# A Fourier mixing layer with a feed-forward block: the first unit's transform by direct tables, and folds at other steps

## The chip, the cores and the metric

The kernel runs on one core of a Trainium2 chip. The metric is the device time of one execution in microseconds (us). In the text, TensorE is the matrix engine (PE in the profile, PEld its weight loads), DVE the vector engine, ACT the scalar engine, GpSimd is POOL, and SyncE (SP) issues the transfers.

## The reference

The input `x` has 8 samples of 3008 rows and 256 columns. A two-dimensional Fourier transform is taken per sample, its real part goes through two matrix products with a leaky ReLU between them.

```python
X = np.fft.fft(x, axis=1)              # x: (8, 3008, 256)
X = np.fft.fft(X, axis=2)
x = X.real.astype(np.float32).reshape(24064, 256)
h = x @ w_in                           # w_in: (256, 2048)
g = np.maximum(0.01 * h, h)
out = (g @ w_out).astype(np.float32)   # w_out: (2048, 256)
```

The kernel gets the weights as 64-bit floats and converts them itself (`begin`, `mantissa`, `end`: bit operations on DVE and ACT).

## The kernel before

The transform along the 3008 rows uses symmetries. Rows are laid out in 8 chunks of up to 95 rows (`ROWS`), each beside its mirror image, in two halves `h`. The *folds* add and subtract mirrored rows and columns, so that a small matrix of cosines or sines remains. A *unit* is one sample `b` and one parity `c` of the output frequencies; there are 16 units, the first is `(0, 1)`. Each unit has two parts: cosines (part 0) and sines (part 1). The column in the middle of the features (the Nyquist column) is treated apart, for all 8 samples at once.

```python
def add_mirrors(t, h, rows):
    a, z = t[:, h, 0, rows], t[:, h, 1, rows]
    nc.vector.tensor_tensor(a, a, z, op=ALU.add)

def fold_columns(t, h, part, rows, v=nc.vector):
    a, z = t[:, h, 0, rows], t[:, h, 1, rows]
    if part == 0:
        nc.vector.tensor_tensor(z[:, :, 0:P], a[:, :, 0:P], a[:, :, P:D], op=ALU.add)
    else:
        v.tensor_tensor(z[:, :, P + 1 : D], a[:, :, 1:P], a[:, :, P + 1 : D], op=ALU.subtract)
        nc.gpsimd.memset(z[:, :, P : P + 1], 0.0)

def fold_halves(t, part, c, rows, to=None, v=nc.vector):     # one halving
    ...
    v.tensor_tensor(to, z[:, 0], z[:, 1], op=(ALU.add, ALU.subtract)[i])

def fold_x(b, h):                       # a later sample, one half of it
    add_mirrors(t, h, rows)
    for part in range(2):
        fold_columns(t, h, part, rows)
    if h == 1:
        for part in range(2):
            for c in PARITIES:
                fold_halves(t, part, c, rows)
```

For parity 1 a further fold needs *turns*: pairs of chunks are turned by an angle, which is two or four scalings on ACT and two sums on DVE or GpSimd.

```python
def turn(x, y, a, part, tmp, to, v):
    nc.scalar.activation(tmp[0], y, ACT.Copy, scale=sin)
    nc.scalar.activation(tmp[1], y, ACT.Copy, scale=cos)
    if v is nc.vector:
        v.scalar_tensor_tensor(to[0], in0=x, scalar=cos, in1=tmp[0], op0=ALU.mult, op1=op[part])
        v.scalar_tensor_tensor(to[1], in0=x, scalar=sin, in1=tmp[1], op0=ALU.mult, op1=op[1 - part])
        return
    nc.scalar.activation(to[0], x, ACT.Copy, scale=cos)
    nc.scalar.activation(to[1], x, ACT.Copy, scale=sin)
    v.tensor_tensor(to[0], to[0], tmp[0], op=op[part])
    v.tensor_tensor(to[1], to[1], tmp[1], op=op[1 - part])
```

After the folds, `even_rows` and `odd_rows` multiply four chunks each with a table of 95 columns per chunk into a bank of the sum memory (PSUM), and `butterfly` on DVE puts the banks together into `mix`, the transformed block of 752 columns that the first matrix product reads.

The opening, for the first unit (cut):

```python
w = load_w_in(0, half)
nc.sync.dma_start(nyx, x_nyq)
nc.sync.dma_start(angle, angle_tab)
load_rows(0, evens)                    # a quarter of the sample, 1 MB
for n in range(2):
    load_tab(n, 1)
load_rows(1, evens)
for h in range(2):
    load_rows(h, odds)
nc.sync.dma_start(feat_sb, ...)
for n in range(2, 4):
    load_tab(n, 1)
o = load_w_out(0)
convert(w)
fold_nyquist()
nyq = nyquist_rows(1)
...
add_mirrors(t, 0, evens)
fold_columns(t, 0, 0, evens)
fold_columns(t, 0, 1, evens, nc.gpsimd)
keep_warm(17)                          # matmuls on zeroes
nyq = mix_nyquist(nyq, nc.gpsimd)
... # the other folds, turns and products, on DVE, GpSimd and ACT
fold_halves(t, 1, 1, odds, v=nc.gpsimd)
sine.fold_odd(nc.gpsimd)
...
even, odd = mix(units[0], 1)
even(even_sines)
odd(odd_rows(sine, P))
o.begin()
o.mantissa()
```

After the opening come steps. A step `(j, f)` takes a chunk of 251 columns of `mix` through two blocks of hidden columns: `up` (four matmuls, then DVE and ACT make `g`), and three steps later `down` (seven matmuls with sums made by GpSimd; at the chunk's last `f`, seven adds on DVE that empty the four sum banks). Between them the folds and transforms of the unit to come are put in:

```python
if 0 < n < len(units) - 1:
    ...
    if part == 0 and n % 2 == 1 and f in (2, 5):
        fold_x(b + 1, f // 5)
    if part > 0 and f == 1:
        fold_rows(units[n + 1], part - 1)
    if part > 0 and f == 4:
        dft(units[n + 1], part - 1)
...
if at - lag >= done:
    down(*steps[at - lag])             # lag = 3
```

Of the kernel before, what the change touches and what calls it, by code (L numbers as in the profile page):

```python
# [53 lines left out]
F32 = mybir.dt.float32  # L56
# [6 lines left out]
P = 128  # L63
# [11 lines left out]
KB = [47, 94]  # L75

PARITIES = (1, 0)

# [51 lines left out]
def seq_tables():  # L130

    out = np.zeros((4, 2, P, TW[0][1]), np.float32)
    rows = row_order()

# [18 lines left out]
    for part in range(2):  # L153
# [19 lines left out]
        out[2 * part + 1, 0, :, : TW[0][1]] = np.concatenate([values(4, fours)[part], values(4, eights)[part], p, q], axis=1)  # L173
    return out

# [51 lines left out]
def tile_fnet_leaky_relu(  # L227
# [5 lines left out]
    w_out: bass.AP,  # L233
    seq_tab: bass.AP,
    angle_tab: bass.AP,
    feat_tab: bass.AP,
# [13 lines left out]
    def dft_ps():  # L250
        return up_ps("dft_ps")
# [13 lines left out]

    def fold_columns(t, h, part, rows, v=nc.vector):

        a, z = t[:, h, 0, rows], t[:, h, 1, rows]
        if part == 0:
            nc.vector.tensor_tensor(z[:, :, 0:P], a[:, :, 0:P], a[:, :, P:D], op=ALU.add)  # L270
        else:
            v.tensor_tensor(z[:, :, P + 1 : D], a[:, :, 1:P], a[:, :, P + 1 : D], op=ALU.subtract)  # L272
            nc.gpsimd.memset(z[:, :, P : P + 1], 0.0)

    def fold_halves(t, part, c, rows, to=None, v=nc.vector):

        i, cols = (c + part) % 2, slice(part * P, (part + 1) * P)
        z = t[:, :, 1, rows, cols]
        to = t[:, i, 0, rows, cols] if to is None else to[:, rows]
        v.tensor_tensor(to, z[:, 0], z[:, 1], op=(ALU.add, ALU.subtract)[i])  # L280

    def fold_x(b, h):

        t, rows = xs[b], slice(0, NT)
        add_mirrors(t, h, rows)
        for part in range(2):
            fold_columns(t, h, part, rows)
        if h == 1:
            for part in range(2):
                for c in PARITIES:  # L290
                    fold_halves(t, part, c, rows)
            zs[b] = xs.pop(b)
# [56 lines left out]
    def rows_of_x(b, part, c):  # L349

        t = zs[b]
        src = t[:, (c + part) % 2, 0, :, part * P : (part + 1) * P]
        return Rows(src, [t[:, part, 1].rearrange("p c (i d) -> p (c i) d", i=2)], part, c)


# [171 lines left out]

    def butterfly(to, m, part, c, v=nc.vector):

# [15 lines left out]

        banks = []

        def copied(bank, at, w):

            banks.append(bank)  # L550
            a = work.tile([P, 384], F32, tag="e0", bufs=2, name="e0")
            if v is nc.vector:
                nc.scalar.copy(a[0:m, 0:w], bank[0:m, at : at + w])
                return a, bank
            used = 4 * ROWS if bank is banks[0] else 4 * n + 2
            nc.scalar.copy(a[0:m, 0:used], bank[0:m, 0:used])
            return a[:, at:], a

        def even(pe):
            if c == 1:  # L560
                e0, pe = copied(pe, 0, 2 * ROWS)
                x, y = two(e0, 0, ROWS, ROWS), two(pe, 2 * ROWS, ROWS, ROWS)
                v.tensor_tensor(four(ab)[:, 0::2], x[:, :, 1:], y[:, :, 1:], op=ALU.add)
                either(four(ab)[:, 1], x[:, 0, 1:], y[:, 0, 1:])
                v.tensor_tensor(four(ab)[:, 3], x[:, 1, 0:n][:, ::-1], y[:, 1, 0:n][:, ::-1], op=ALU.subtract)
                v.tensor_tensor(ev[0:m, 0 : 2 * n], ab[0:m, 0 : 2 * n], ab[0:m, 2 * n : 4 * n], op=ALU.add)
                either(ev[0:m, 2 * n : 4 * n], ab[0:m, 0 : 2 * n], ab[0:m, 2 * n : 4 * n])
                return
# [6 lines left out]

        def odd(po):
            if c == 1:
                q = 2 * n + 1
# [5 lines left out]
                return  # L584
            direct = od[0:m, n : n + 378].rearrange("p (a n) -> p a n", a=2)[:, :, 0:188]
            nc.scalar.copy(direct.rearrange("p a (b n) -> p b a n", b=2)[:, :, :, 0:48],
                           po[0:m, 0:192].rearrange("p (b a n) -> p b a n", b=2, a=2))
# [11 lines left out]

    def mix(u, blk):  # L600

        t = work.tile([P, UW[0]], F32, tag=f"mix{blk}", bufs=2, name=f"mix{blk}")
        mixed.setdefault(u, {})[blk] = t
        return butterfly(t, P, blk, u[1])

# [14 lines left out]

    def nyquist_rows(c):
        rows = Rows(nya[:, c], [nyz], 0, c)
        rows.fold_even(nc.gpsimd)
        rows.fold_odd(nc.gpsimd)
        return rows

    def mix_nyquist(rows, v):
        c = rows.c
        banks = even_rows(rows, B), odd_rows(rows, B)
        t = work.tile([P, UW[0]], F32, tag="mix0", bufs=2, name="nyq")  # L630
        for made, bank in zip(butterfly(t, B, 0, c, v), banks):
            made(bank)
        nc.sync.dma_start(nyq_dram[:, c, 0 : UW[c]], t[0:B, 0 : UW[c]])
        return t
# [116 lines left out]
    def step(at):  # L751
        if at < len(steps):
# [6 lines left out]
            if 0 < n < len(units) - 1:  # L759
                if part == 0 and f == 4:  # L760
                    spread(units[n + 1])
                if part == 0 and n % 2 == 1 and f in (2, 5):
                    fold_x(b + 1, f // 5)
                if part > 0 and f == 1:
                    fold_rows(units[n + 1], part - 1)
                if part > 0 and f == 4:
                    dft(units[n + 1], part - 1)
# [14 lines left out]
    with tc.manual_schedule(engines={mybir.EngineType.DVE, mybir.EngineType.PE, mybir.EngineType.SP}):  # L782
        with tc.manual_schedule(engines={mybir.EngineType.Pool, mybir.EngineType.Activation}):
# [16 lines left out]
            w = load_w_in(0, half)  # L800
            nc.sync.dma_start(nyx, x_nyq)
            nc.sync.dma_start(angle, angle_tab)
            load_rows(0, evens)
            for n in range(2):
                load_tab(n, 1)
            load_rows(1, evens)
            for h in range(2):
                load_rows(h, odds)
            nc.sync.dma_start(feat_sb, feat_tab.rearrange("(a p) n -> p a n", p=P))
            for n in range(2, 4):  # L810
                load_tab(n, 1)
            o = load_w_out(0)
            convert(w)
            fold_nyquist()
            nyq = nyquist_rows(1)

            def blocks_of(tag, name):
                return work.tile([P, 2 * WN], F32, tag=tag, bufs=dict(s=4, g=5)[tag], name=name).rearrange("p (c d) -> p c d", d=P)

            differences = blocks_of("s", "differences")  # L820
            cosine, sine = (Rows(src, [blocks_of("g", "folded") for _ in range(2)], part, 1)
                            for part, src in enumerate((differences, t[:, 0, 0, :, P:D])))
            add_mirrors(t, 0, evens)
            fold_columns(t, 0, 0, evens)
            fold_columns(t, 0, 1, evens, nc.gpsimd)
            keep_warm(17)
            nyq = mix_nyquist(nyq, nc.gpsimd)
            add_mirrors(t, 1, evens)
            fold_columns(t, 1, 0, evens)
            fold_columns(t, 1, 1, evens)  # L830
            fold_halves(t, 0, 1, evens, differences)
            cosine.fold_even()
            fold_halves(t, 1, 1, evens)
            keep_warm(8)
            even_cosines = even_rows(cosine, P)
            sine.fold_even(nc.gpsimd)
            for h in range(2):
                add_mirrors(t, h, odds)
                fold_columns(t, h, 0, odds)
                fold_columns(t, h, 1, odds, (nc.vector, nc.gpsimd)[h])  # L840
            fold_halves(t, 0, 1, odds, differences)
            cosine.fold_odd()
            fold_w_in(0, half, w, "sum")
            w, w1 = load_w_in(half, half), load_w_in(WN, WN)
            even_sines = even_rows(sine, P)
            even, odd = mix(units[0], 0)
            even(even_cosines)
            fold_halves(t, 1, 1, odds, v=nc.gpsimd)
            sine.fold_odd(nc.gpsimd)
            zs[0] = t  # L850
            odd_cosines = odd_rows(cosine, P)
            odd(odd_cosines)
            spread_first(nyq)
            even, odd = mix(units[0], 1)
            even(even_sines)
            odd(odd_rows(sine, P))
            o.begin()
            o.mantissa()
            nyq = nyquist_rows(0)
        with tc.manual_schedule(engines={mybir.EngineType.Activation}):  # L860

# [3 lines left out]
            o1 = load_w_out(1)  # L865
            for n in range(4):
                load_tab(n, 0)
            up(*steps[1])
# [50 lines left out]
        for part in range(2):  # L919
            fold_rows(units[1], part)  # L920
    mix_nyquist(nyq, nc.vector)
    spread(units[1])
# [35 lines left out]
```

## Time and profile before

| | |
|---|---|
| time, median of 3 | 1918.74 us (1918.53 to 1919.8) |
| profiled span | 1917.6 us |
| busy TensorE, DVE, GpSimd, ACT | 1898.6, 1293.5, 1136.7, 514.1 us |
| mean granted TensorE clock | 0.994 |
| moved by transfers | 76.01 MB, mean 40 GB/s |

Lines of the profile name the line of the kernel (L672), the engine, the operation, what is written and read (out<-in), and a count (x4). A note in brackets tells the idle time before the instruction and what ended it. In a timeline the first two numbers are start and duration in us. In a list of waits they are the total, the number of times and the longest wait. In the kernel before, L264 is `add_mirrors`, L270 and L272 `fold_columns`, L280 `fold_halves`, L298 to L307 the turns, L524 the products of the transform, L582 and L583 the two last instructions of `mix` for the first unit, L672 the matmuls of `up`, L735 those of `down`, L746 the seven adds and L780 the matmuls on zeroes. A matmul on 32-bit floats has two records.

### The profile page before, as it was taken

The page shows a single profiled execution, that of the slowest core. Times are in us where ns is not written, and L with a number is a line of the kernel's source. Part 1 is how long each engine was busy: PE and PEld are TensorE (multiplying, and loading weights), DVE is VectorE, ACT ScalarE, POOL GpSimd, SP SyncE. Part 2 cuts the span into 40 slices and gives each one's busy share as a digit, 9 for nine tenths or more (in the row PEclk, how much of TensorE's full clock was granted, in tenths as well). Part 3 has the DMA queues.
Part 4 walks back from the last instruction along what each step waited for, and adds up shares of the span by engine and source line. Part 5 has one row for each costly group of instructions (what it writes and reads, how often), then busy time and mean ns, then how long its engine had stood idle before and what let it go on. Part 6 is the DMA issues. An engine that isn't in the chain of part 4 may idle for free.

```text
span 1917.6 us, 25461 instructions
## 1 busy us (share of the span) xinstructions
PE 1898.6 (99%) x9132; PEld 1689.9 (88%) x9132; DVE 1293.5 (67%) x2580; ACT 514.1 (27%) x721; POOL 1136.7 (59%) x1551
## 2 busy tenths in 40 slices
PE   8999999999999999999999999999999999999999
PEld 6789888888889888888888988889888888888988
DVE  7878855697556966569655796558864587556554
ACT  4532322222222322223222232222322222222221
POOL 5117655576555865558655675557655576555554
PEclk7999999999999999999999999999999999999999
DMA  5313000020001100020000200002000030000000
GB/s 190 104 31 118 12 20 12 22 107 12 20 22 59 60 12 31 12 99 20 18 25 12 107 12 23 19 12 107 22 12 20 11 118 12 20 12 22 11 11 22
DMA packets 26876, 76.01 MB, mean 40 GB/s; under 512 B 4976, under 2 KB 18672, under 8 KB 24960
## 3 DMA queue, kind: packets, MB, share of 16 engines
q1 hardware_dynamic: 25600, 74.40, 10.4%
q8 instruction: 73, 1.20, 0.3%
q14 instruction: 51, 0.42, 0.1%
q10 hardware_dynamic: 1152, 0.00, 0.0%
HBM read 49.68 MB, written 24.71 MB: 39 GB/s over the span
## 4 chain that ended last, share of the span: by engine, by line
PE 92%; DVE 4%; issue 1%; DMA 0%; ACTq 0%; ACT 0%; DVEq 0%; SPq 0%
PE sum_ps L735 54%; PE cos_ps L672 16%; PE sin_ps L672 16%; PE dft_ps L524 3%; PE sum_ps L715 2%; DVE g L681 1%; DVE cos L677 1%; DVE g L682 1%; DVE xt L280 1%; DVE xt L272 0%; DMA xt<-in_x_dram 0%; PE wf_ps L468 0%; DVE xt L264 0%; DVE e L746 0%; ACTq L477 0%
## 5 line engine op out<-in xcount | busy, mean ns | idle before, releaser
L683 ACT ACTIVATE g<-g 128x1004 f32<-128x1004 f32 (+1 forms) x384 | 399.3, 1040 | 1096.1 <-DVE g L682 1022.6
L677 DVE SCALAR_TENSOR_TENSOR cos<-nb,wn,cos_ps 128x251 f32<-128x251 f32 (+1 forms) x768 | 329.6, 470 | 522.4 <-PE cos_ps L672 521.8
L690 POOL TENSOR_TENSOR s<-g 128x251 f32<-128x251 f32 (+1 forms) x368 | 283.5, 770 | 659.5 <-ACT g L683 659.5
L735 PE MATMUL sum_ps<-s,wt 128*128 128x251 f32 (+1 forms) x2208 | 529.0, 374 | 3.3 <-DVE e L746 3.3
L735 PEld LDWEIGHTS sum_ps<-s,wt 128*128 128x128 f32 x2208 | 415.4, 188 | 57.5 <-issue 5.3
L672 PE MATMUL cos_ps<-mix,wf 128*128 128x251 f32 (+1 forms) x1536 | 391.0, 376 | 1.8 <-ACT wf L470 1.8
L672 PE MATMUL sin_ps<-mix,wf 128*128 128x251 f32 (+1 forms) x1536 | 388.8, 375 | 0.2 <-DVE mix L582 0.2
L735 PE MATMUL sum_ps<-g,wo 128*128 128x251 f32 (+1 forms) x1472 | 373.1, 375 | 0.5 <-DVE o L746 0.5
L672 PEld LDWEIGHTS cos_ps<-mix,wf 128*128 128x128 f32 x1536 | 292.0, 190 | 36.9 <-ACT wf L470 2.8
L672 PEld LDWEIGHTS sin_ps<-mix,wf 128*128 128x128 f32 x1536 | 291.1, 190 | 35.9 <-PE cos_ps L672 0.8
L691 POOL TENSOR_TENSOR s<-s,g 128x251 f32<-128x251 f32 (+1 forms) x368 | 318.6, 866 | 0.0
L735 PEld LDWEIGHTS sum_ps<-g,wo 128*128 128x128 f32 x1472 | 276.9, 190 | 32.7 <-DVE o L746 1.3
L693 POOL TENSOR_TENSOR s<-g,s 128x251 f32<-128x251 f32 (+1 forms) x368 | 279.7, 760 | 28.9
L681 DVE TENSOR_TENSOR g<-cos,sin_ps 128x502 f32<-128x502 f32 (+1 forms) x384 | 259.4, 675 | 44.5 <-DVE cos L677 8.0
L682 DVE TENSOR_TENSOR g<-cos,sin_ps 128x502 f32<-128x502 f32 (+1 forms) x384 | 257.0, 669 | 0.0
L692 POOL TENSOR_TENSOR s<-g 128x251 f32<-128x251 f32 (+1 forms) x368 | 251.0, 682 | 0.0
L735 PE MATMUL sum_ps<-g,wt 128*128 128x251 f32 (+1 forms) x736 | 215.8, 375 | 0.0
L735 PE MATMUL sum_ps<-s,wo 128*128 128x251 f32 (+1 forms) x736 | 215.8, 375 | 0.0
L735 PEld LDWEIGHTS sum_ps<-s,wo 128*128 128x128 f32 x736 | 139.4, 189 | 16.4
L735 PEld LDWEIGHTS sum_ps<-g,wt 128*128 128x128 f32 x736 | 139.8, 190 | 15.8
L746 DVE TENSOR_TENSOR o<-e,sum_ps 128x251 f32<-128x251 f32 (+1 forms) x184 | 67.4, 408 | 8.7 <-ACT e L744 8.7
L524 PEld LDWEIGHTS dft_ps<-tab,xt 95*128 95x128 f32 x484 | 59.2, 192 | 1.6
(133 smaller groups left out, 892.3 us busy)
## 6 DMA issues: line engine op xcount, KB each, us to landing
xt<-in_x_dram SPq DMA_DIRECT2D x14, 2048.0 KB, 9.8
out_dram<-o SPq DMA_DIRECT2D x80, 251.0 KB, 2.3
xt<-in_x_dram SPq DMA_DIRECT2D x4, 1024.0 KB, 9.5
raw<-in_w_out_dram SPq DMA_DIRECT2D x8, 512.0 KB, 4.4
out_dram<-o SPq DMA_DIRECT2D x16, 250.0 KB, 2.2
raw<-in_w_in_dram SPq DMA_DIRECT2D x6, 512.0 KB, 5.0
nb<-nyq_dram SPq DMA_DIRECT2D x8, 376.5 KB, 3.4
nb<-nyq_dram SPq DMA_DIRECT2D x7, 376.0 KB
```

Source lines behind the costliest of these rows:

```text
L524: nc.tensor.matmul(o, lhsT=still, rhs=moving, start=(i == 0), stop=(i == 3), skip_group_check=True)
L672: nc.tensor.matmul(pt[blk][:, h * n : (h + 1) * n], lhsT=wf[:, blk, fs[h] * P : (fs[h] + 1) * P], rhs=mixed[b, c][blk][:, at : at + n], st ...
L677: nc.vector.scalar_tensor_tensor(cos[:, hs], in0=spreads[b, c][:, at : at + n], scalar=wn[:, fs[h] : fs[h] + 1], in1=pt[0][:, hs], op0=ALU ...
L681: nc.vector.tensor_tensor(g[:, 0], cos[:, 0 : 2 * n], pt[1][:, 0 : 2 * n], op=ALU.add)
L682: nc.vector.tensor_tensor(g[:, 1], cos[:, 0 : 2 * n], pt[1][:, 0 : 2 * n], op=ALU.subtract)
L683: nc.scalar.activation(g, g, ACT.Lrelu)
L690: nc.gpsimd.tensor_tensor(s1, a[1][0], a[1][1], op=ALU.add)
L691: nc.gpsimd.tensor_tensor(s2, s1, a[0][0], op=ALU.subtract)
L692: nc.gpsimd.tensor_tensor(s3, a[0][0], a[1][0], op=ALU.subtract)
L693: nc.gpsimd.tensor_tensor(s4, a[0][1], s2, op=ALU.subtract)
L735: nc.tensor.matmul(sums[j][p], lhsT=still[p], rhs=moving[p], start=(f == 0 and i % 2 == 0), stop=(f == NH - 1), skip_group_check=True)
L746: nc.vector.tensor_tensor(to, x, y, op=ALU.add)
```

## The change

The first unit and its part of the Nyquist column are transformed without turns: new tables (`direct_tab`, 1.06 MB for each part) hold full cosines and sines for each chunk, so the folded chunks go straight to TensorE. All folds of `x` run on DVE; the zeroing of a column that is zero already goes. The loads are reordered: the tables come in three pieces between the quarters of `x`, the old tables of parity 1 are loaded later. More matmuls on zeroes keep TensorE running. For later samples the folds are put at other steps, away from the step in which a chunk ends. The aim is a shorter opening with TensorE at full clock, and no waits for the seven adds.

```diff
+    class Direct:
+        def even_rows(self, m):
+            pe, n, at = dft_ps(), KB[1], 0                      # KB[1] = 94
+            for i, (lo, hi) in enumerate(((0, n), (n, 2 * n), (2 * n, 4 * n), (2 * n, 4 * n))):
+                nc.tensor.matmul(pe[0:m, lo:hi], lhsT=self.src[:, i], rhs=self.tab[0][0:ROWS, at : at + hi - lo],
+                                 start=(i == 0), stop=(i == 3), skip_group_check=True)
+                at += hi - lo
+            return pe
+        def odd_rows(self, m):
+            po, n = dft_ps(), KW[1]                             # KW[1] = 376
+            for i in range(4):
+                nc.tensor.matmul(po[0:m, 0:n], lhsT=self.src[:, 4 + i], rhs=self.tab[1 + i // 2][0:ROWS, i % 2 * n : (i % 2 + 1) * n],
+                                 start=(i == 0), stop=(i == 3))
+            return po
... # butterfly with direct=True: even()
+                e0, pe = copied(pe, 0, n)
+                v.tensor_tensor(ab[0:m, 0:n], e0[0:m, 0:n], pe[0:m, n : 2 * n], op=ALU.add)
+                either(ab[0:m, n : 2 * n], e0[0:m, 0:n], pe[0:m, n : 2 * n])
+                v.tensor_tensor(ev[0:m, 0 : 2 * n], ab[0:m, 0 : 2 * n], pe[0:m, 2 * n : 4 * n], op=ALU.add)
+                either(ev[0:m, 2 * n : 4 * n], ab[0:m, 0 : 2 * n], pe[0:m, 2 * n : 4 * n])
... # and odd(): no copy on DVE's side
+                v.tensor_tensor(to[0:m, 0:kw], ev[0:m, 0:kw], po[0:m, 0:kw], op=ALU.add)
+                v.tensor_tensor(to[0:m, kw : UW[c]], ev[0:m, 0:kw], po[0:m, 0:kw], op=ALU.subtract)
... # fold_columns
-            nc.gpsimd.memset(z[:, :, P : P + 1], 0.0)
... # fold_x, h == 1: the four halvings go, and in step:
-                if part == 0 and n % 2 == 1 and f in (2, 5):
+                if part == 0 and n % 2 == 1 and f in (3, 5):
                     fold_x(b + 1, f // 5)
-                if part > 0 and f == 1:
+                if n % 2 == 1 and (part, f) in ((0, 7), (1, 0)):
+                    for i in range(2):
+                        fold_halves(zs[b + 1], i, 1 - part, slice(0, NT))
+                if part > 0 and f == 3:
                     fold_rows(units[n + 1], part - 1)
-                if part > 0 and f == 4:
+                if part > 0 and f == 5:
                     dft(units[n + 1], part - 1)
... # the opening's loads
+            for h in range(2):
+                load_rows(h, evens)
+            load_direct(0, (0,))                                # first piece, 0.29 MB
+            load_rows(0, odds)
+            nc.sync.dma_start(feat_sb, feat_tab.rearrange("(a p) n -> p a n", p=P))
+            load_direct(0, (1, 2))                              # 0.77 MB
+            load_rows(1, odds)
+            load_direct(1, range(3))                            # 1.06 MB
             nc.sync.dma_start(angle, angle_tab)
             o = load_w_out(0)
... # and its folds and products
+            for h in range(2):
+                add_mirrors(t, h, evens)
+                fold_columns(t, h, 0, evens)
+                fold_columns(t, h, 1, evens)
             fold_halves(t, 0, 1, evens, differences)
             fold_halves(t, 1, 1, evens)
             for h in range(2):
                 add_mirrors(t, h, odds)
                 fold_columns(t, h, 0, odds)
+                if h == 0:
+                    fold_columns(t, h, 1, odds)
             fold_halves(t, 0, 1, odds, differences)
+            fold_columns(t, 1, 1, odds)
+            fold_halves(t, 1, 1, odds)
+            keep_warm(24)
+            even_nyq = nyq.even_rows(B)
+            keep_warm(5)
+            even_cosines = cosine.even_rows(P)
             fold_w_in(0, half, w, "sum")
             w, w1 = load_w_in(half, half), load_w_in(WN, WN)
+            nyq = mix_nyquist(1, (even_nyq, nyq.odd_rows(B)), nc.gpsimd)
+            even, odd = mix(units[0], 0, direct=True)
+            even(even_cosines)
+            even_sines = sine.even_rows(P)
+            odd(cosine.odd_rows(P))
+            even, odd = mix(units[0], 1, direct=True)
+            even(even_sines)
+            odd_sines = sine.odd_rows(P)
             spread_first(nyq)
+            odd(odd_sines)
... # after the first step
-            for n in range(4):
-                load_tab(n, 0)
+            for c in range(2):
+                for n in range(4):
+                    load_tab(n, c)
```

## The prediction

> **What bounds the kernel now.** I read the page's busy table first, then the waits of TensorE after the opening, then the opening in the table of windows and in the timeline, and last the timeline around one place where TensorE waited.
>
> ```profile
> span 1917.6 us, 25461 instructions
> ...
> PE 1898.6 (99%) x9132; PEld 1689.9 (88%) x9132; DVE 1293.5 (67%) x2580; ACT 514.1 (27%) x721; POOL 1136.7 (59%) x1551
> ```
>
> TensorE is busy 99% of the span, so two things only can shorten it: the opening, before TensorE has real work, and places where TensorE stands later. The waits of TensorE from 100 us to the end are two lines, 3.8 us together:
>
> ```profile
> PE sum_ps L735 <- DVE e L746: 3.3, 5, 0.8
> PE sum_ps L735 <- DVE o L746: 0.5, 1, 0.5
> ```
>
> Cut up place by place they are 0.3 us near 418 us, 0.8 us at each of four later samples and 0.5 us at one more; the first sample (near 185 us) has none. That is the ceiling for the second half of the change. The rest of its gain must come from the opening. The table of windows for it (columns: start and end of the window, length, busy us and count by engine, granted clock, DMA share, GB/s):
>
> ```profile
> 8.00:12.00 4.00, 4.00 (x30) 3.25 (x28) 1.92 (x2) 0.99 (x4) 3.54 (x6) 1.00 1.04 418
> 16.00:18.00 2.00, 1.04 (x6) 0.82 (x6) 1.53 (x3) 0.69 (x2) 1.84 (x4) 1.00 1.06 367
> 18.00:22.00 4.00, 4.00 (x12) 3.10 (x12) 2.06 (x4) 1.28 (x4) 2.18 (x4) 0.58 0.36 123
> 22.00:26.00 4.00, 1.37 (x9) 1.02 (x7) 3.93 (x5) 0.00 (x0) 2.28 (x4) 0.93 0.00 0
> 26.00:30.00 4.00, 0.24 (x1) 0.27 (x2) 3.50 (x8) 2.24 (x8) 2.14 (x3) 0.50 0.00 0
> ...
> 36.00:42.00 6.00, 5.83 (x16) 4.42 (x16) 5.39 (x15) 2.64 (x8) 0.22 (x2) 0.50 0.04 12
> ```
>
> The transfers run at about 400 GB/s and are over by 20 us; then DVE, ACT and GpSimd work on for almost 20 us while TensorE is idle and its granted clock falls to 0.50. The timeline tells what they do; the rows that carry the argument (start, duration):
>
> ```profile
> 9.01 1.23 DVE L264 TENSOR_TENSOR xt<-xt 128x1024 f32<-128x1024 f32 x1 [1.90 <-DMA xt<-in_x_dram]
> 12.59 1.22 DVE L264 TENSOR_TENSOR xt<-xt 128x1024 f32<-128x1024 f32 x1 [1.62 <-DMA xt<-in_x_dram]
> ...
> 19.93 0.69 DVE L280 TENSOR_TENSOR xt<-xt 128x512 f32<-128x512 f32 x1 [1.91 <-POOL xt L273]
> ...
> 26.68 1.54 POOL L280 TENSOR_TENSOR xt<-xt 128x512 f32<-128x512 f32 x1
> ...
> 33.63 1.03 POOL L338 TENSOR_TENSOR folded<-folded 95x256 f32<-95x256 f32 x1
> ...
> 34.71 2.02 PE L524 MATMUL dft_ps<-tab,folded 95*128 95x95 f32 x8 [0.16 <-POOL folded L338]
> ...
> 37.93 0.55 DVE L582 TENSOR_TENSOR mix<-ev,od 128x376 f32<-128x376 f32 x1
> 38.40 0.54 DVE L583 TENSOR_TENSOR mix<-ev,od 128x376 f32<-128x376 f32 x1
> ...
> 38.63 2.01 PE L672 MATMUL sin_ps<-mix,wf 128*128 128x251 f32 x4 [0.17 <-DVE mix L582]
> ```
>
> The first unit's transform ends with `mix` at 38.94 us. Its last part goes through GpSimd (26.68), the turns on ACT and GpSimd (to 34.66), TensorE (34.71), then DVE. From there DVE stays the pace: its busy time is 18.65 of the 20 us from 40 to 60 and 34.26 of the 40 us to 100 (converting the weights), and its only waits up to 60 us are 0.53 us for a small transfer and 0.20 us for TensorE. So if `mix` is ready earlier by d, I expect all that follows, and the end, to come earlier by d.
>
> **What the Trainium skill says.** "TensorE: Matmul & The Clock Gate", Part 1: the array runs at half rate until it has been busy for a window of some 3.4 us, and falls back after an idle one. This trace agrees: 0.50 in the windows after the idle stretch from 24 to 29.7 us, 1.00 from 44 us. "SBUF — State Buffer", Who interferes with whom: a DVE instruction with two SBUF inputs and a GpSimd instruction that reads SBUF take one shared interface by turns. It agrees: the 128x512 halving on DVE took 0.69 us alone and 1.63 us beside GpSimd. "GPSIMD Engine Reference", 4.1: two-input elementwise work is about twice as slow there; here the 128x508 fold took 0.82 us on DVE and 1.76 us on GpSimd. "DMA: Bandwidth & Descriptors", Specifications: a fabric ceiling of 435 GB/s; the trace's best window of 2 us has 420, so the longer load can't be had faster.
>
> **The change, part by part.**
>
> *Loads.* Bytes in the order of the queue, in MB. Before, up to the last piece of x: weights 0.52, the Nyquist column 0.13, x 4 x 1.05, two tables 0.38: 5.23, and that piece landed near 17.7 us (issued at about 5.9, the longest of the four landings is 11.8). The second piece stood at 3.13 and was waited for until 12.59. This gives 2.10 MB in 5.1 us, 0.41 MB/us. After: the second piece stands at 0.65 + 2.10 = 2.75, so 12.59 - 0.38/0.41 = 11.7 us; the first direct table at 3.04 (12.4); the third piece at 4.09 (15.0); feature table and the rest of the first direct table at 5.12 (17.5); the last piece at 6.17 (20.1); the second direct table at 7.23 (22.7). The change thus brings the last x about 2.3 us later, and the direct tables cost 2.12 MB in place of 0.77 MB.
>
> *Folds.* Each quarter of x costs 1.22 + 0.70 + 0.82 us on DVE, a halving 0.69 us without GpSimd beside it. First quarter from 9.0 to 11.8; second to 14.5; two halvings to 15.9; third to 18.6; then DVE waits for the last piece until 20.1. After it: 1.22 + 0.70 + 0.69 + 0.82 + 0.69 = 4.1, so 24.2. GpSimd now has just the 8-row Nyquist mix, six instructions of 0.3 to 0.97 us (3.5 us), which start when ACT has copied (about 20.6) and fall just beside these folds; I add 0.6 us for the shared interface: 24.8.
>
> *Turns.* Before, 18 ACT turns of about 0.39 us on the two parts (and 12 of 8 columns for the Nyquist rows), with their DVE and GpSimd products: gone from the path. In their place TensorE takes 94+94+188+188 columns for the even rows and 4 x 376 for the odd ones, in place of 380 and 378. A column costs two records of 1/1.2 ns at full clock (251 columns: 0.2125 us a record, 5.10 us for 24), so the odd rows take 2.5 us and the even ones 0.94 us. Odd cosines can start when their halving ends (about 23.3) and end at 25.8; odd sines end at 28.3.
>
> *Is the clock full there?* Warm matmuls: 48 records; the old 34 lasted to 10.5, 14 more of 0.213 reach 13.5. Then Nyquist evens 14.4, five more warm ones 16.6, cosine evens 17.5, the weight fold (8 records of 256) 19.3, Nyquist odds 21.8, sine evens 22.8 (their table lands at 20.8). No gap of a microsecond until the odd cosines: I take the full clock.
>
> *Mix.* DVE after its last fold: four even instructions (two of 0.25, two of 0.35 us: 1.2), two of 0.55 for the first `mix` (27.1), 1.2 for the even sines (28.3), then the second `mix` 28.4 to 29.5. No ACT copy of the odd bank is left. `mix` is ready at 29.5 in place of 38.94: **9.4 us**. The weights for the next conversions are issued once the first fold of `w_in` is copied (near 20 us); with 1.6 MB behind 7.75 MB they land near 26.5 us and are wanted at 31.
>
> *Later folds.* Before, from the second sample on, the halving of the next sample stands between the seven adds that free the sum banks:
>
> ```profile
> 416.85 1.22 DVE L280 TENSOR_TENSOR xt<-xt 128x1024 f32<-128x1024 f32 x1
> ...
> 418.54 1.09 PE L735 MATMUL sum_ps<-s,wt 128*128 128x251 f32 x4 [0.25 <-DVE e L746]
> ```
>
> In the changed program's order of DVE the adds come before two of the halvings at all seven samples, as they do now at the first sample only, where TensorE didn't wait. Two halvings (2 x 1.14 us of spacing) move behind the adds, and the whole fold starts a step (4.66 us) later, which also covers the wait for x (14.2 us at L264 in nine places, 3.5 of it in the opening). I expect 3.5 of the 3.8 us back. The zeroing on GpSimd that goes (0.11 us each, 14 times) lies off the path.
>
> Sum: 1918.7 - 9.4 - 3.5 = **1905.8 us**, 0.7% faster.
>
> **The rivals.** *The load becomes the bound.* For it: DVE already waits for x, the queue moves 400 GB/s and 1.35 MB are added. If the last piece lands at 23 us instead of 20.1, everything behind moves with it: about 1908.7. Against it: the tables after it have 3 us to spare. *TensorE falls to half clock.* If a table comes late and leaves it idle, odd rows of 5 us each put `mix` at about 33 to 34 us, and the end near 1910. Against it: the added warm matmuls. *The gain is absorbed.* If the stretch from 39 to 100 us waits for weight transfers and not for DVE, half of the 9.4 us would be left: 1910. Against it: DVE's waits above, and the windows from 40 to 44 us in which the queue moves nothing. *More than I count.* Before, TensorE ran at 0.50 until 43 us; if it set part of the pace there, another 1 to 2 us come: 1904. *New waits later:* the transform is one step nearer to its fold's end (two steps in place of three); the fold for the transform at 459.74 us ended on DVE at 440.28, four steps before, so a step less should do.
>
> **Range and chances.** Opening 6 to 11.5 us, later folds 2 to 4: 1903 to 1910.5. The 2% line is 38 us, three times the estimate and twice the whole opening before `mix`, so faster by over 2% has 0.01; slower by 38 us would need a stall of a microsecond at every fifth step: 0.01; within 2%: 0.98.
>
> **What would show it.** Right: `mix` done near 29.5 us; granted clock 1.00 from 10 to 44 us; DVE waiting some 1.5 us for the last piece of x near 20 us; TensorE's waits on `e` and `o` after 100 us under 0.5 us. Wrong: a DVE wait for x of over 3 us, a wait of TensorE for a direct table, new waits of DVE on raw weights between 30 and 60 us, or TensorE waiting for `mix` or the transform at a unit's start.

## The result and the profile after

The changed kernel takes 1905.72 us (median of 4 runs, 1905.13 to 1905.83) against 1918.77 us before: the ratio is 0.993, with a 95% interval of 0.9913 to 0.9948. The profiled spans are 1904.0 and 1917.6 us. The prediction was 1905.8 us.

The page of the kernel after, the same lines as before:

```profile
span 1904.0 us, 25360 instructions
...
PE 1895.9 (100%) x9140; PEld 1688.2 (89%) x9140; DVE 1283.4 (67%) x2569; ACT 504.1 (26%) x689; POOL 1122.5 (59%) x1511
```

The work of TensorE is the same within 3 us, and its share is 100%: what went is idle time. From 90 us to the end the list of its waits is empty. In the kernel after, L274 is `add_mirrors`, L281 and L283 `fold_columns`, L290 `fold_halves`, L372 and L380 the even and odd rows by the direct tables, L612 and L613 the last instructions of `mix`, L702 `up`, L707 the first DVE instruction behind it, L765 `down`, L776 the seven adds.

The table of windows of the kernel after (window, length, busy us and count of PE, PEld, DVE, ACT and POOL, granted clock, DMA share, GB/s):

```profile
0.00:8.00 8.00, 6.90 (x23) 5.82 (x24) 3.48 (x12) 3.41 (x6) 2.22 (x9) 1.00 0.67 196
8.00:12.00 4.00, 4.00 (x20) 3.51 (x20) 1.36 (x2) 0.00 (x0) 0.00 (x0) 1.00 0.98 383
...
18.00:22.00 4.00, 4.00 (x18) 2.24 (x17) 1.85 (x4) 1.10 (x3) 0.77 (x2) 1.00 1.03 406
22.00:26.00 4.00, 3.57 (x16) 2.09 (x15) 3.90 (x5) 0.70 (x2) 3.84 (x4) 1.00 1.00 338
26.00:30.00 4.00, 4.00 (x14) 2.21 (x13) 3.69 (x11) 0.24 (x1) 2.65 (x8) 1.00 0.55 203
```

Where the old kernel had no transfers and a TensorE that was idle for most of the time (22 to 30 us, with the clock at 0.50 from 26 us on), the new one keeps both busy and the clock is 1.00. The timeline of the kernel after (start, duration):

```profile
10.61 1.23 DVE L274 TENSOR_TENSOR xt<-xt 128x1024 f32<-128x1024 f32 x1 [3.34 <-DMA xt<-in_x_dram]
...
13.96 1.12 PE L372 MATMUL dft_ps<-direct,nyx 95*8 95x94 f32 x8 [0.37 <-DMA direct<-in_direct_tab_dram]
...
21.48 1.23 DVE L274 TENSOR_TENSOR xt<-xt 128x1024 f32<-128x1024 f32 x1 [2.12 <-DMA xt<-in_x_dram]
...
23.49 0.95 DVE L290 TENSOR_TENSOR differences<-xt 128x512 f32<-128x512 f32 x1
...
24.59 2.76 PE L380 MATMUL dft_ps<-direct,differences 95*128 95x376 f32 x8 [0.43 <-DVE differences L290]
...
25.46 1.35 DVE L290 TENSOR_TENSOR xt<-xt 128x512 f32<-128x512 f32 x1
...
27.19 2.69 PE L380 MATMUL dft_ps<-direct,xt 95*128 95x376 f32 x8
...
30.03 0.55 DVE L612 TENSOR_TENSOR mix<-ev,dft_ps 128x376 f32<-128x376 f32 x1
30.50 0.54 DVE L613 TENSOR_TENSOR mix<-ev,dft_ps 128x376 f32<-128x376 f32 x1
```

The path is now: the last quarter of x lands (21.48), its folds and the halving of the differences, two sets of odd rows one after the other on TensorE (24.59 to 29.88), the last two instructions of `mix`. It is ready at 31.04 us in place of 38.94.

To see where the 13.6 us between the spans arise, I compared the start of each of ACT's 384 activations (one for each `up`, in the same order in both kernels). How much earlier the kernel after is:

| activation, its time before | earlier by |
|---|---|
| 1st, 42.8 us | 7.93 us |
| 11th, 100.8 us | 8.11 us |
| 51st, 299.0 us | 8.12 us |
| 99th, 530.4 us | 8.62 us |
| 147th, 762.3 us | 9.67 us |
| 195th, 994.2 us | 10.72 us |
| 303rd, 1514.8 us | 11.89 us |
| 375th, 1861.0 us | 13.64 us |

In this pair of traces the opening is worth 8.1 us and then nothing changes until 300 us; the other 5.5 us come in jumps of 0.1 to 1.8 us, at the folds of the later samples.

### The profile page after: what moved, and what is told of

Its sections match the earlier page's. It is cut to its first block, busy times and chain, and to the rows that moved or that the text cites. A ratio compares the mean times of both kernels' runs of the same rounds, so it can differ in the third digit from the quotient of the medians.

```text
span 1904.0 us, 25360 instructions
## 1 busy us (share of the span) xinstructions
PE 1895.9 (100%) x9140; PEld 1688.2 (89%) x9140; DVE 1283.4 (67%) x2569; ACT 504.1 (26%) x689; POOL 1122.5 (59%) x1511
## 4 chain that ended last, share of the span: by engine, by line
PE 97%; DVE 1%; DMA 1%; SPq 0%; issue 0%; ACTq 0%; ACT 0%; DVEq 0%
PE sum_ps L765 57%; PE cos_ps L702 17%; PE sin_ps L702 17%; PE dft_ps L553 3%; PE sum_ps L745 2%; DMA xt<-in_x_dram 1%; PE wf_ps L497 0%; PE dft_ps L380 0%; DVE cos L707 0%; ACTq L506 0%; ACT wf L499 0%; DVE g L711 0%; DVE g L712 0%; SPq L843 0%; DVE power L462 0%
## 5 line engine op out<-in xcount | busy, mean ns | idle before, releaser
L707 DVE SCALAR_TENSOR_TENSOR cos<-nb,wn,cos_ps 128x251 f32<-128x251 f32 (+1 forms) x768 | 330.3, 470 | 524.7 <-PE cos_ps L702 524.1
L765 PE MATMUL sum_ps<-s,wt 128*128 128x251 f32 (+1 forms) x2208 | 527.6, 374 | 0.0
L765 PEld LDWEIGHTS sum_ps<-s,wt 128*128 128x128 f32 x2208 | 415.9, 188 | 52.4
L702 PE MATMUL cos_ps<-mix,wf 128*128 128x251 f32 (+1 forms) x1536 | 388.3, 375 | 1.8 <-ACT wf L499 1.8
L702 PE MATMUL sin_ps<-mix,wf 128*128 128x251 f32 (+1 forms) x1536 | 387.6, 374 | 0.0
L765 PE MATMUL sum_ps<-g,wo 128*128 128x251 f32 (+1 forms) x1472 | 372.9, 375 | 0.0
L702 PEld LDWEIGHTS cos_ps<-mix,wf 128*128 128x128 f32 x1536 | 290.9, 190 | 37.0 <-ACT wf L499 2.8
L702 PEld LDWEIGHTS sin_ps<-mix,wf 128*128 128x128 f32 x1536 | 290.4, 189 | 34.7
L765 PEld LDWEIGHTS sum_ps<-g,wo 128*128 128x128 f32 x1472 | 277.3, 190 | 31.5
L765 PE MATMUL sum_ps<-g,wt 128*128 128x251 f32 (+1 forms) x736 | 215.8, 375 | 0.0
L765 PE MATMUL sum_ps<-s,wo 128*128 128x251 f32 (+1 forms) x736 | 215.8, 375 | 0.0
L765 PEld LDWEIGHTS sum_ps<-s,wo 128*128 128x128 f32 x736 | 139.4, 189 | 16.4
L765 PEld LDWEIGHTS sum_ps<-g,wt 128*128 128x128 f32 x736 | 139.8, 190 | 15.8
L776 DVE TENSOR_TENSOR o<-e,sum_ps 128x251 f32<-128x251 f32 (+1 forms) x184 | 67.5, 408 | 8.7 <-ACT e L774 8.7
```

The costliest lines, as they stand in the source:

```text
L702: nc.tensor.matmul(pt[blk][:, h * n : (h + 1) * n], lhsT=wf[:, blk, fs[h] * P : (fs[h] + 1) * P], rhs=mixed[b, c][blk][:, at : at + n], st ...
L707: nc.vector.scalar_tensor_tensor(cos[:, hs], in0=spreads[b, c][:, at : at + n], scalar=wn[:, fs[h] : fs[h] + 1], in1=pt[0][:, hs], op0=ALU ...
L765: nc.tensor.matmul(sums[j][p], lhsT=still[p], rhs=moving[p], start=(f == 0 and i % 2 == 0), stop=(f == NH - 1), skip_group_check=True)
L776: nc.vector.tensor_tensor(to, x, y, op=ALU.add)
```

## The experiments

The kernel before, run again on the chips of the experiments, spread from 1916.26 to 1920.95 us, so differences of one or two microseconds between kernels are read from the marks in the traces (activations as above), and the times stand beside them. A mark belongs to one execution. At the 11th activation four traces with the changed opening (the kernel after, `e1`, `e3`, `e4`) are 8.1 to 8.5 us earlier than before; the later marks hold waits that differ more, as shown below.

### The later folds by themselves

`e1_old_later` is the changed kernel with all the later folds at their old steps; `e2_later_only` is the kernel before with them at the new ones.

```diff
 # e1: in the kernel after
-                if part == 0 and n % 2 == 1 and f in (3, 5):
+                if part == 0 and n % 2 == 1 and f in (2, 5):
-                if n % 2 == 1 and (part, f) in ((0, 7), (1, 0)):   # halvings: back into fold_x
-                if part > 0 and f == 3:
+                if part > 0 and f == 1:
-                if part > 0 and f == 5:
+                if part > 0 and f == 4:
 # e2: the reverse, in the kernel before
```

> The changed opening with the later folds of the kernel before. By the mark-by-mark comparison of the two traces the opening is worth 8.1 us and the later folds 5.5: then 1918.7 - 8.1 = 1910.6, and the waits of TensorE for the seven adds are back (about 3.8 us in the list). Rival, the prediction's own split (opening 9.4, later folds 3.5): 1909.3.

Measured: 1908.75 us (1908.12 to 1909.01), ratio to before 0.9947 (0.9932 to 0.9962). At 100.8 us it is 8.54 us earlier than before, at 1861 us 10.45. By its time it is faster than either expectation.

> The kernel before with only the later folds at the new steps. If TensorE loses more at those places than its listed waits of 3.8 us: 1918.7 - 5.5 = 1913.2. If the listed waits are all that there is to gain (the prediction's ceiling): 1914.9 or more.

Measured: 1914.41 us (1914.04 to 1916.12), ratio 0.9978 (0.9969 to 0.9987). It is 0.23 us later than before at 100.8 us and 4.93 us earlier at 1861: 5.2 us from the later folds alone, with no listed wait of TensorE. The time (4.4 us faster by the medians) is between the two expectations and its interval holds both; the marks are for the larger. Either half of the change gains without the other. `e1_old_later` gains 1.9 us more between the two marks although it has the old later folds, so its places cost less than before's. The list of its TensorE's waits from 100 us on:

```profile
PE sum_ps L768 <- DVE e L779: 2.2, 6, 0.8
```

Six waits again, but 2.2 us in place of 3.8.

### Which of the moved steps does it

The change moves four things: the folds of x, the halvings, the folds of rows, and the next unit's transform (`dft`). The order of DVE's instructions is made by a scheduler, and the changed program's order shows one thing that the diff doesn't: it depends on the transform's step. With `dft` at `f == 4` DVE's order is the old one, with the other three at their old or at their new steps; with `f == 5` it is the new one in both cases. The traces agree: from the 11th activation on, DVE's instructions stand in one order in all five kernels with `f == 4` and in another in all six with `f == 5`.

```diff
 # e3_all_but_transform, in the kernel after
-                if part > 0 and f == 5:
+                if part > 0 and f == 4:
                     dft(units[n + 1], part - 1)
 # e4_transform_step_only: the kernel after with f in (2, 5), no moved halvings, fold_rows at f == 1; dft stays at f == 5
```

> The changed kernel with the transform of the next unit back at f == 4; the folds of x, the halvings and the folds of rows stay at their new steps. The order of DVE's instructions is then the same as with all the old steps. Theory A (what moves the halvings behind the adds is the transform's step alone): the later gain is gone, 1911.2, as e1. Theory B (the prediction's: moving the folds and halvings themselves does it): the gain stays, 1905.7 to 1907.

Measured: 1909.6 us (1908.41 to 1910.05), ratio 0.9951 (0.9936 to 0.9966). That is between the two theories, nearer to A. From 100.8 us to 1861 us it gains 1.0 us over before, where the kernel after gains 5.5. Its list of waits:

```profile
PE sum_ps L765 <- DVE e L776: 3.0, 6, 0.8
```

> The changed kernel with the folds of x, the halvings and the folds of rows back at their old steps; only the transform is at f == 5. Theory A: the whole later gain stays, 1905.7. Theory B: it goes, about 1911.

Measured: 1905.38 us (1905.28 to 1906.06), ratio 0.9931 (0.9914 to 0.9947). Between the two marks it gains 5.5 us, the same as the kernel after, and TensorE has no listed wait. Theory A holds: the transform's step is the cause; the three other moves together do nothing to the time beside it.

Why it should act on the folds shows in the waits of SyncE's queue (from 100 us to the end). First the kernel before, then the kernel after:

```profile
SPq L256 <- PE dft_ps L524: 48.4, 7, 11.8
```

```profile
SPq L266 <- PE dft_ps L553: 78.0, 7, 11.7
```

L256 and L266 are the load of the next sample. There is one buffer for x, and the load waits for the last product of the transform that still reads it. A transform one step later means a load one step later: the seven waits grow by 29.6 us, 4.2 us each, near the step's 4.66. `e4_transform_step_only` has 78.3 us in this list and `e3_all_but_transform` 49.7. The fold starts when the data lands: the first fold of the second of these samples starts at 392.43 us before and at 388.69 us after, which is 4.4 us later once the opening's 8.1 us are taken off. That the scheduler comes to its new order by way of this buffer fits these numbers; no run moves the load alone.

The place itself, in the timeline of the kernel after, where the prediction showed 416 to 419 us of the kernel before:

```profile
407.78 0.41 DVE L776 TENSOR_TENSOR e<-e,sum_ps 128x250 f32<-128x250 f32 x1
408.49 0.48 DVE L707 SCALAR_TENSOR_TENSOR cos<-nb,wn,cos_ps 128x251 f32<-128x251 f32 x1 [0.30 <-PE cos_ps L702]
408.88 0.73 DVE L776 TENSOR_TENSOR e<-e,sum_ps 128x250 f32<-128x250 f32 x2
409.53 1.05 DVE L776 TENSOR_TENSOR o<-e,sum_ps 128x250 f32<-128x250 f32 x3
...
410.89 1.21 DVE L290 TENSOR_TENSOR xt<-xt 128x1024 f32<-128x1024 f32 x1
```

No halving stands between the adds, DVE even waits for TensorE among them (0.30 us), and three halvings follow. So it is at all six samples at which the orders differ: before, three halvings ahead of the seven adds and the fourth behind the second of them; after, one ahead and three behind.

### More is lost at a wait than the list says

The prediction took the listed waits, 3.8 us, as the most that could be had. Loss against the kernel after, from the marks at 100.8 and 1861 us:

| kernel | listed waits of TensorE on the adds | lost by the marks |
|---|---|---|
| before | 3.8 us in 6 | 5.5 us |
| all but the transform | 3.0 us in 6 | 4.5 us |
| changed opening, old later folds | 2.2 us in 6 | 3.6 us |
| turns, folds on DVE (`e7`, below) | 2.5 us in 4 | 3.9 us |
| old opening at full clock (`e8`, below) | 2.4 us in 5 | 3.9 us |
| only the later folds | none | 0.4 us |
| transform's step only | none | 0.0 us |

In the five kernels with waits the loss is 1.4 to 1.7 us above the list, some 0.25 to 0.35 us for each wait. A part of that is in how the profile draws matmuls: their ends are modelled, one of 251 columns has 0.375 us on average although they follow one another each 0.2125 us, so the record before a gap covers 0.16 us of it. The remaining 0.1 us or more isn't explained by these runs.

The same five kernels have the same order of DVE's later instructions, and lose from 3.6 to 5.5 us, the kernel before the most. So 5.5 us is the loss of one execution. The medians on one chip give less: the later gain is 4.4 us with the old opening (before against `e2_later_only`), and 4.2 and 3.4 us with the new one (`e3` and `e1` against `e4`). The opening is worth 9.0 us there (`e2` against `e4`).

### What in the opening does it: turns, GpSimd, or the clock

`e7_dve_folds_turns` keeps the turns and moves only the opening's folds from GpSimd to DVE.

```diff
 # in the kernel before
-            fold_columns(t, 0, 1, evens, nc.gpsimd)
+            fold_columns(t, 0, 1, evens)
-                fold_columns(t, h, 1, odds, (nc.vector, nc.gpsimd)[h])
+                fold_columns(t, h, 1, odds)
-            fold_halves(t, 1, 1, odds, v=nc.gpsimd)
+            fold_halves(t, 1, 1, odds)
-            nc.gpsimd.memset(z[:, :, P : P + 1], 0.0)
```

> The kernel before, turns and all, with only the folds of x in the opening moved from GpSimd to DVE (and without the zeroing). If the turns are the cost: mix is ready at most 2 us earlier, 1916.7 to 1919.7. If GpSimd's folds were the cost: half of the 8 us or more, 1914.7 or less.

Measured: 1920.11 us (1918.56 to 1921.21), ratio 1.0005 (0.9997 to 1.0014): no gain, and slower than either expectation. By the first activation of its trace it is 2.77 us later; its first quarter of x was already late (taken up at 10.67 us, 9.01 in the kernel before). Its timeline:

```profile
31.84 0.69 DVE L280 TENSOR_TENSOR xt<-xt 128x512 f32<-128x512 f32 x1
...
37.49 2.02 PE L524 MATMUL dft_ps<-tab,folded 95*128 95x95 f32 x8 [2.81 <-POOL folded L338]
```

The sines' last halving (0.69 us) now stands in DVE's queue behind the cosines' even rows, 5 us after GpSimd did it before, and the turns on ACT and GpSimd still follow it: 5.65 us from its start to the product. So this run doesn't give the sines an earlier halving, and is a weak test of GpSimd's share.

`e8_warm_before` keeps TensorE busy in the old opening.

```diff
 # in the kernel before
+            keep_warm(14)
             odd_cosines = odd_rows(cosine, P)
...
+            keep_warm(4)
             odd(odd_rows(sine, P))
```

> The kernel before with 18 more matmuls on zeroes in TensorE's idle stretches of the opening (14 before the odd cosines, 4 before the odd sines). If the clock is a small part: 1 to 2 us, since on the path only about 2 us of products run at half clock: 1916.7 to 1917.7. Rival, the opening's gain is mainly the full clock: 1914.7 or less.

Measured: 1918.5 us (1917.83 to 1919.32), ratio 0.9996 (0.9987 to 1.0004). By its median it is 0.6 us faster than the kernel before, less than both expectations. The windows and three lines of its timeline:

```profile
32.00:36.00 4.00, 3.58 (x16) 2.25 (x14) 3.11 (x6) 2.21 (x8) 3.86 (x8) 1.00 0.99 325
36.00:40.00 4.00, 2.90 (x17) 2.38 (x16) 3.86 (x12) 0.62 (x2) 0.82 (x5) 1.00 0.11 44
```

```profile
20.76 0.69 DVE L280 TENSOR_TENSOR xt<-xt 128x512 f32<-128x512 f32 x1 [1.91 <-POOL xt L273]
...
35.57 1.13 PE L524 MATMUL dft_ps<-tab,folded 95*128 95x95 f32 x8 [0.42 <-POOL folded L338]
...
38.45 0.54 DVE L583 TENSOR_TENSOR mix<-ev,od 128x376 f32<-128x376 f32 x1
```

The clock is full, the odd sines take 1.13 us in place of 2.02, and `mix` is ready at 38.99 us, where it was at 38.94. This execution was 0.83 us behind at its second halving (20.76 against 19.93), ahead of the added matmuls, and made that up: the full clock is worth some 0.8 us.

What is left are the turns, and the traces before and after show them. In the kernel before, 6.49 us pass from the end of the last halving of the sines (26.68 + 1.54) to their product at 34.71: turns on ACT and GpSimd. In the kernel after it is 0.38 us (25.46 + 1.35 to 27.19). That is 6.1 of the 7.9 us. Of the rest, the halving ends 1.4 us earlier, the product with the direct table takes 0.7 us longer (2.69 against 2.02), and from its end `mix` takes 1.16 us in place of 2.21. No run has the tables alone, so this split is read from two traces and not from an experiment.

`e6_gpsimd_folds` puts three folds of the changed kernel back on GpSimd, and `e5_no_warm` takes its matmuls on zeroes away.

```diff
 # e6, in the kernel after
-                fold_columns(t, h, 1, evens)
+                fold_columns(t, h, 1, evens, (nc.gpsimd, nc.vector)[h])
-            fold_columns(t, 1, 1, odds)
-            fold_halves(t, 1, 1, odds)
+            fold_columns(t, 1, 1, odds, nc.gpsimd)
+            fold_halves(t, 1, 1, odds, v=nc.gpsimd)
 # e5, in the kernel after
-            keep_warm(24)
+            keep_warm(1)
-            keep_warm(5)
```

> The changed kernel with three folds back on GpSimd: the second column fold of the first quarter, and of the last quarter with its halving. If having all folds on DVE is a main part of the opening's gain: 2 us or more slower, 1907.7 or more. If the turns are the main part: the sines' last halving comes about 1 to 2 us later but the odd cosines on TensorE cover most of it, 0 to 1.5 us slower.

Measured: 1907.41 us (1906.83 to 1914.34), ratio 0.9946 (0.993 to 0.9963); 1.56 us later than the kernel after at the 11th activation. One of its five runs took 1914.34, the others 1907.41 at most. It lies between the two expectations, near the second. Its timeline shows the halving of the differences at 1.64 us beside GpSimd's fold of 1.77 us; in the kernel after it took 0.95:

```profile
22.70 1.77 POOL L283 TENSOR_TENSOR xt<-xt 128x508 f32<-128x508 f32 x1 [9.24 <-DMA angle<-in_angle_tab_dram]
23.39 1.64 DVE L290 TENSOR_TENSOR differences<-xt 128x512 f32<-128x512 f32 x1
```

GpSimd's fold starts where DVE's add of the mirrors ends (22.63 us); the transfer in its note is not one that it reads.

> The changed kernel with 1 matmul on zeroes in place of the 24 and without the 5 after the Nyquist evens. If those matmuls are what keeps the clock full for the odd rows: the odd rows take up to twice their 2.6 us and the first mix comes 2 us or more later, 1907.7 or more. Rival: the real products from 14 us on bring the clock up in time, under 0.7 us.

Measured: 1906.79 us (1906.36 to 1907.64), ratio 0.9935 (0.9921 to 0.995); 0.88 us later by the 11th activation. Between the two expectations, nearer to the rival: the odd rows still took 2.69 us each, so the clock was full by then. The products ahead of them took about twice as long (even rows 2.04 and 2.48 us in place of 1.12 and 1.25, the fold of `w_in` 3.62 in place of 1.89); the odd cosines started at 25.60 in place of 24.59 us. The matmuls on zeroes are worth about a microsecond.

### The order of the loads

`e9_x_first` loads the last quarter of x ahead of the feature table and of two pieces of the first direct table.

```diff
             load_rows(0, odds)
+            load_rows(1, odds)
             nc.sync.dma_start(feat_sb, ...)
             load_direct(0, (1, 2))
-            load_rows(1, odds)
             load_direct(1, range(3))
```

> The changed kernel with the last quarter of x loaded ahead of the feature table and of the last two pieces of the first direct table. If the landing of the last piece of x sets the pace (the prediction's view): it lands about 2.5 us earlier and mix comes up to 2 us earlier, 1903.7 to 1905. If TensorE's products set it as much (they have 2.6 us for each set of odd rows and stand in one queue): the Nyquist odds wait for their table until about 21.5 us and mix comes 0.5 to 1.5 us later, 1906.2 to 1907.2.

Measured: 1906.06 us (1905.96 to 1906.31), ratio 0.9935 (0.9919 to 0.9952); 0.49 us later at the 11th activation than the kernel after. The first expectation fails; this is the lower end of the second. Its timeline:

```profile
19.07 1.22 DVE L274 TENSOR_TENSOR xt<-xt 128x1024 f32<-128x1024 f32 x1
...
21.43 2.69 PE L380 MATMUL dft_ps<-direct,nyx 95*8 95x376 f32 x8
...
27.77 2.69 PE L380 MATMUL dft_ps<-direct,xt 95*128 95x376 f32 x8
```

DVE no longer waits and takes the last quarter up 2.4 us earlier, but the Nyquist odds start at 21.43 in place of 20.18 us and all of TensorE's queue behind them with it. This order moves the tables as well as x, so it doesn't show what an earlier x would give by itself. The trace of the kernel after limits that: its odd cosines waited 0.43 us for the halving, and the odd sines followed them without a wait. TensorE and the load of x are within half a microsecond of each other; `mix` at about 31 us is where both end.

## Why the prediction was right, and where it was not

The time was met (1905.8 against 1905.72), in part by luck: of its two terms one was too large and the other too small. Predicted were 9.4 + 3.5 us; measured are 8.1 + 5.5 between the two traces, and 9.0 + 4.4 by the medians on one chip. Two of the signs that the prediction named for being wrong are there: DVE waited over 3 us for x (3.34 us for the first quarter, 1.90 before), and TensorE waited for a direct table (0.37 us at 13.96 us).

*Shift of the opening carried to the end: right.* `mix` came 7.90 us earlier, the first activation 7.93, the 11th 8.11, and this stayed until 300 us. The rival that weight transfers absorb half of it falls.

*Size of the opening: too large by 1.5 us in this trace.* `mix` was ready at 31.04 us and not at 29.5; in the three other traces with this opening and only other later folds it is 30.6. The term at fault is the landings. The last quarter of x was taken up at 21.48 us (21.0 to 21.2 in those three) where 20.1 was predicted, the first direct table at 13.96 in place of 12.4, so DVE and TensorE's queue were late together. The prediction took the old queue's times over. From 0 to 8 us the new queue moved 196 GB/s and the old one 240, then 383 against 418 until 12 us: 0.35 + 0.14 MB less, which at 0.41 MB/us is 1.2 us. The first quarter shows it too: 10.61 us in place of 9.01. Not all of this is the new order: with the old one the first quarter was taken up at 9.0 to 10.7 us in four traces, with the new one at 10.0 to 10.6 in seven, so the prediction had worked from a fast one. The rival "the load becomes the bound" was half right: the wait for the last piece is 2.12 us, not 1.5, but TensorE's queue would have set nearly the same end.

*Products, clock, shared interface: right in the main.* The odd rows took 2.6 us a set (2.5 predicted), the clock was 1.00, the folds after the last piece ended at 26.8, 5.3 us after its landing (4.7 predicted, GpSimd's six instructions lay beside them as said). "SBUF — State Buffer" of the Trainium skill, Who interferes with whom, has it that the two engines take the shared interface by turns; the 1.35 and 0.95 us halvings here, 1.64 in `e6_gpsimd_folds` and 0.69 alone agree. What the prediction read of the clock's rule in the old trace goes too far: its own windows have 0.58 from 18 to 22 us, ahead of the idle stretch, and 0.50 from 36 to 42 us with TensorE listed as busy for 5.83 of the 6 us. They give no length for the window.

*Gain of the later folds: too small, by 2 us in these two traces and by up to 0.9 us by the medians.* The listed waits are not a ceiling: each costs some 0.25 to 0.35 us more than listed. A slip in reading them changes nothing in the sum: the wait of 0.5 us isn't at a sample of its own but beside one of 0.8 (1576 and 1578 us), and the sample near 1345 us has none.

*Its mechanism: half right.* That halvings go behind the adds is what the new order and the timeline show, three at each of six samples and not two at seven. The step that failed is "the whole fold starts a step (4.66 us) later, which also covers the wait for x". The fold does start later, but the prediction lets this follow from the folds' new steps and doesn't name the transform's. Without the transform's new step the other moves change nothing in DVE's order, and the transform's step alone gives the whole gain. The data comes a step later too, so the wait for x is not covered: outside the opening DVE waited 10.7 us in seven places before and 8.7 us after.

*The rival "more than I count"* (the half clock until 43 us set part of the pace): with the full clock in the old opening the time moved by a ratio of 0.9996, so no. *New waits later*: none.

## What to carry to other kernels

Where a scheduler orders an engine's queue, test which of several moved lines changes that order before giving any of them the credit; here one number of four did, probably through a buffer that a load had to wait for. When an opening moves from waiting engines to a full transfer queue, allow for landings that differ by a microsecond or more from one execution to the next, and more so where the queue's order changes. A short list of waits of a saturated engine can fall short of what they cost, here by 1.4 to 1.7 us; compare marks along the two traces to get the loss itself, and take more than one trace, since the same order of instructions lost 3.6 us in one and 5.5 in another.

## What was not expected of the hardware

An instruction of only 8 rows on GpSimd is held up beside DVE as well: in the kernel after, 8 rows of 94 columns took 0.34 us when they started ahead of DVE's fold and 1.37 us beside it; in `e6_gpsimd_folds`, where they came later, both took 0.34. And the transfers are slow to reach their rate with either order: 196 to 240 GB/s over the first 8 us, of which the first two moved 31 GB/s at most, and 405 to 410 from 12 to 16 us.
